# Loading keys and values through two DMA queues in a decode attention block

## The chip, the cores and the metric

The kernel runs on one core of a Trainium2 chip. The core has five engines that run side by side, each with its own stream of instructions: TensorE (PE, matrix products into PSUM), VectorE (DVE), ScalarE (ACT), GpSimd (POOL) and SyncE (SP, which here only issues transfers). Sixteen DMA engines move data between the chip's memory (HBM) and the core's on-chip memory (SBUF, 128 partitions). Instructions wait for each other through semaphores. A transfer raises its semaphore by 16 when it has landed. The metric is the device time of one execution in microseconds.

## The reference

A batch of four tokens goes through attention over cached keys and values and through a small mixer in parallel, and all is summed.

```python
xn = layernorm(x)                                   # x: (4, 1, 512)
q  = xn @ wq, cut into heads# (4, 32 heads, 1, 128)
scores = einsum("bhqd,bhkd->bhqk", q, k_cache) * 128 ** -0.5
o  = einsum("bhqk,bhkd->bhqd", softmax(scores), v_cache) -> (4, 1, 4096) @ wo
out = x + attention(xn) + mixer(xn)                 # mixer: xn + gelu(layernorm(xn) @ w3) @ w4
```

(Only one token stands in each sequence, so the mixer's shifts leave nothing of its first two matrices.) `k_cache` and `v_cache` have the shape (4, 32, 4096, 128) in float32: 268 MB each, read once. All other inputs together are about 24 MB. There is hardly any arithmetic for each byte.

## The kernel before

The 128 pairs of batch and head are worked in 32 **groups** of four heads (`NG = 32`, `HG = 4`). A group's keys are 8 MiB, laid out as 128 rows of 64 KiB, one row for each partition: partitions 0 to 31 hold the first head's keys, and so on. Its values have the same layout. SBUF holds three such slots: `KS[0]` and `KS[1]` take the keys of even and odd groups in turn, `S2` takes the values of every group. `S2` also holds, before the loop, the weights `wq`; `KS[1]` (`S0`) holds the layer norm's intermediates before that, so that its first keys wait for `d_T`, the signal that the queries `Q` are ready.

What each engine does for a group, in a loop of its own:

- **VectorE** spreads the group's queries over the partitions (L337, L340), waits for the keys (`s_k[n]`), multiplies them by the query in two halves (L343, L345), sums each product over the 128 elements (L347), then signals `k_free`, takes the maximum (L349 to L352) and signals `d_a`. For the first group the second half of the keys is a load of its own, and L345 waits for it (`s_h`, passed on by GpSimd).
- **ScalarE** waits for `d_a` and takes the exponentials, four instructions and their sums (`weights`, L245), which TensorE waits for (`a_p`). It then waits for TensorE's products and copies them out of PSUM (`values`, L233), waits for the sums and copies the group's result (`outputs`, L253). Its loop takes one group a turn; in the last turn it also has two instructions of the mixer (L261, L264).
- **TensorE** waits for the values (`s_v`) and the exponentials and makes 32 products with the values as moving operand, then signals `v_free` with the first product of the sums.
- **SyncE** issues every load but that of x (which ScalarE issues), in the order of its stream: `wq` in two pieces (L127, L128), the first group's keys in two halves (L130), then, after `d_T`, K1 (L119), V0 (L123), K2, V1, K3 and so on: each K load after `k_free`, each V load after `v_free`. At the end come `w3` (L146), `w4` (L148, L153), the last values in two pieces (L150, L152) and `wo` in six pieces (L157).

A transfer that is issued waits for nothing more; it stands in its queue behind those that the same engine issued earlier. The semaphores of the loads are taken back to zero by the one who waits (`take`), so each counts one load at a time. The names K*g* and V*g* below are the keys and values of group *g*.

Of the kernel before, what the change touches and what calls it, by code (L numbers as in the profile page):

```python
# [20 lines left out]
def decode_block(ctx: ExitStack, tc: tile.TileContext, x, k, v, wq, wo, w3, w4, out):  # L21
# [48 lines left out]
    def take(e, s, n=1):  # L70
        e.wait_ge(s, n).then_inc(s, -n)  # L71
# [26 lines left out]
    V = S2[:, :].rearrange("p (a j h d) -> p a h j d", a=C // 16, j=4, h=4)  # L98
    wo_sb = S0[:, :].rearrange("p (c n) -> p c n", c=WC)

    def part(t):
        return slice(t * P, (t + 1) * P)

# [7 lines left out]
    with tc.tile_critical(no_gpsimd_drain=True), nc.Block(no_gpsimd_drain=True) as block:  # L111

        @block.sync
        def _(e):
            def src(flat, g):
                return flat[g] if isinstance(g, int) else flat[bass.ds(g, 1)].rearrange("g p r -> (g p) r")

            def load_k(g, n):
                e.dma_start(KS[n][:, :], src(kf, g)).then_inc(s_k[n], 16)  # L119

            def load_v(g):
                take(e, v_free)
                e.dma_start(S2[:, :], src(vf, g)).then_inc(s_v, 16)  # L123

            FIRST, REST = slice(0, GF * 4 * DH), slice(GF * 4 * DH, ROW)
            wq_r = wq.rearrange("(p c) n -> p (c n)", p=P)
            e.dma_start(S2[:, FIRST], wq_r[:, FIRST]).then_inc(s_v, 16)  # L127
            e.dma_start(S2[:, REST], wq_r[:, REST]).then_inc(s_q, 16)  # L128
            for half, s in ((slice(0, ROW // 2), s_k[0]), (slice(ROW // 2, ROW), s_kh)):
                e.dma_start(S1[:, half], kf[0][:, half]).then_inc(s, 16)  # L130
            e.wait_ge(d_T, 1)
            load_k(1, 1)
            with nc.Fori(0, NG, 2, engines=[ET.SP]) as g:
                load_v(g)
                take(e, k_free)
                e.br_lt(g, NG - 2, on_true="sp_more", on_false="sp_next")
                with nc.body("sp_more", valid_engines=[ET.SP]):
                    after = nc.s_assert_within(g + 2, None, NG - 2,
                                               skip_runtime_bounds_check_because="the last turn skips this block")
                    load_k(after, 0)  # L140
                    load_v(after - 1)
                    take(e, k_free)
                    load_k(after + 1, 1)
                    nc.br("sp_next", engines=[ET.SP])
                nc.switch_bb("sp_next")
            e.dma_start(w3_sb, w3.rearrange("(p c) f -> p c f", p=P)).then_inc(s_w3, 16)  # L146
            w4_r = w4.rearrange("(p m) n -> p m n", p=P)
            e.dma_start(w4_sb[:, 0:4, :], w4_r[:, 0:4, :]).then_inc(s_w4, 16)  # L148
            e.wait_ge(v_half, NG)
            e.dma_start(S2[:, FIRST], vf[NG - 1][:, FIRST]).then_inc(s_v, 16)  # L150
            take(e, v_free)
            e.dma_start(S2[:, REST], vf[NG - 1][:, REST]).then_inc(s_q, 16)  # L152
            e.dma_start(w4_sb[:, 4:NF, :], w4_r[:, 4:NF, :]).then_inc(s_w4, 16)  # L153
            take(e, k_free)
            wo_r = wo.rearrange("(p c) n -> p c n", p=P)
            for n, (c0, c1) in enumerate(PIECES):
                e.dma_start(wo_sb[:, c0:c1, :], wo_r[:, c0:c1, :]).then_inc(s_wo[n], 16)  # L157
# [20 lines left out]
        @block.tensor  # L178
        def _(e):
            pe = [ET.PE]  # L180
            zero = e.zero_reg
            e.br_lt(zero, 0, on_true="pe_near", on_false="pe_far")
            with nc.body("pe_near", valid_engines=pe):
                with nc.Fori(0, NG + 1, 1, engines=pe) as g:
                    e.br_lt(g, NG, on_true="pe_turn", on_false="pe_mlp")
                    with nc.body("pe_mlp", valid_engines=pe):
                        e.wait_ge(s_w3, 16)
                        for c in range(NC):
                            for t in range(4):
                                i = mm(e, pb[32 * t:32 * t + 32, :FT], x1T[:, c, :], w3_sb[:, c, t * FT:(t + 1) * FT],  # L190
                                       c == 0, c == NC - 1)
                        i.then_inc(p_a, 1)
                        nc.br("pe_turn", engines=pe)
                    nc.switch_bb("pe_turn")
                    take(e, s_v, 16)
                    take(e, a_p)
                    for n in range(G4):
                        if n == GF:
                            take(e, v_rest)
                        t = n % 4  # L200
                        i = mm(e, pv[32 * t:32 * t + 32, :], pw[:, n, :], V[:, n // 4, t], n < 4, n >= G4 - 4)
                        if n == GF - 1:
                            i.then_inc(v_half, 1)
                    i.then_inc(p_a, 1)
                    mm(e, oz[:, HG:2 * HG], ones[:, :], rs[:, :], True, True).then_inc(v_free, 1)
                    take(e, a_p)
                    for m in range(4):
                        i = mm(e, oz[:, 0:HG], os[:, m, :], sel[:, HG * m:HG * m + HG], m == 0, m == 3)
                    i.then_inc(p_a, 1)
                e.br_lt(zero, 0, on_true="pe_far", on_false="pe_rest")  # L210
            with nc.body("pe_far", valid_engines=pe):
                e.br_lt(zero, 0, on_true="pe_rest", on_false="pe_near")
            nc.switch_bb("pe_rest")
            mm(e, total[:, 0:P], ident[:, :], base[:, :], True, False)
            e.wait_ge(s_w4, 32)
            take(e, d_p)
            for m in range(NF):
                t = m % 4
                mm(e, y[32 * t:32 * t + 32, :], gT[:, 32 * m:32 * m + 32], w4_sb[:, m, :], m < 4, False)
            take(e, d_p)  # L220
            mm(e, pb[:, 0:P], perm[:, :], Xt[:, :], True, True).then_inc(p_d, 1)

        @block.scalar
        def _(e):
            take(e, g_a)
            e.dma_start(xs[0:B, :], x.rearrange("b s d -> (b s) d")).then_inc(s_x, 16)
            for _ in range(2):
                take(e, d_a)
                e.activation(st[:, 2:3], st[:, 1:2], AF.Sqrt, bias=st[:, 3:4], scale=1.0 / D).then_inc(a_d, 1)

            def values():
                take(e, p_a)
                return e.copy(os[:, :, :], pv[:, :].rearrange("p (m d) -> p m d", m=4)).then_inc(a_p, 1)  # L233

            values()
            e.drain().then_inc(a_d, 1)
            take(e, p_a)
            e.activation(warm[:, :], st[:, 3:4], AF.Exp)

            def weights():  # L240
                take(e, d_a)
                for h in range(HG):
                    r = slice(32 * h, 32 * h + 32)
                    o = pw[r, :, 0:16].rearrange("p (a t) (w h) -> p a t w h", t=4, h=HG)[:, :, :, :, h]
                    i = e.activation(o, sc[r, :].rearrange("p (a w t) -> p a t w", w=4, t=4), AF.Exp, bias=st[r, 1:2], scale=1.0,  # L245
                                     accum_out=rs[r, h:h + 1])
                i.then_inc(a_p, 1)
                e.drain().then_inc(a_d, 1)

            def outputs(o):  # L250
                values()
                take(e, p_a)
                return e.copy(o, oz[:, 0:2 * HG].unsqueeze(1))  # L253

            act = [ET.Activation]
            with nc.Fori(0, NG, 1, engines=act) as g:
                weights()
                e.br_lt(g, NG - 1, on_true="act_values", on_false="act_mlp")
                with nc.body("act_mlp", valid_engines=act):
                    take(e, p_a)  # L260
                    e.copy(hs.rearrange("p (m i) -> p m i", i=32),  # L261
                           pb[:, :FT].rearrange("p (i m) -> p m i", i=32)).then_inc(a_d, 1)
                    take(e, d_a)
                    e.activation(gt, gu, AF.Tanh, scale=GELU_A).then_inc(a_d, 1)  # L264
                    nc.br("act_values", engines=act)
                nc.switch_bb("act_values")
                outputs(OS[:, bass.ds(g, 1), :])
            e.drain().then_inc(a_d, 1)

        @block.vector  # L270
        def _(e):
# [62 lines left out]
            with nc.Fori(0, NG, 2, engines=[ET.DVE]) as g:  # L334
                for n in range(2):
# [2 lines left out]
                                      Q[:, bass.ds(g + n, 1), :].rearrange("p o h -> p (o h)").unsqueeze(2)  # L338
                                      .to_broadcast([P, 4, 32])))
                    own(e.transpose(qb[:, :], qx[:, :]))  # L340
                    take(e, s_k[n], 16)
                    qw = qb[:, :].unsqueeze(1).to_broadcast([P, C // 2, DH])
                    mark(e.tensor_tensor(out=K[:, :C // 2, :], in0=K[:, :C // 2, :], in1=qw, op=ALU.mult))  # L343
                    take(e, s_h)
# [84 lines left out]
```

## Time and profile before

| what | value |
|---|---|
| time, median of 3 runs | 1305.1 us (1304.54 to 1305.36) |
| span of the profiled execution | 1302.8 us |
| the runs' median over that span | 2.3 us |
| DMA traffic | 561.05 MB, 431 GB/s over the span |
| busy: VectorE | 1167.5 us (90%) |
| busy: TensorE, matrix products | 371.5 us (29%) |
| busy: ScalarE | 107.5 us (8%) |

The profile is one execution recorded on the chip. The profiled execution's own time is given as its span, from the first to the last instruction; the times of the runs lie 2.3 us over it. Rows in order of time have the start in us, the duration in us, the engine, the line, the operation, what is written and read, and in brackets how long the engine had been idle and what ended that; SPq and ACTq are the queues of instructions of SyncE and ScalarE, in which a DMA row is the time of issuing and not that of moving the data. DMA queues are numbered: q1 holds what SyncE issues, q10 what ScalarE issues.

### The profile page before, as it was taken

How to read it: one execution, taken by the hardware profiler on the slowest of the kernel's cores; microseconds unless marked ns; L12 is line 12 of the kernel's file. 1: busy time of each engine (PE TensorE's matmuls, PEld its weight loads, DVE VectorE, ACT ScalarE, POOL GpSimd, SP SyncE). 2: the span in 40 equal slices, each digit the busy share in tenths (PEclk: the TensorE clock that was granted, in tenths of full speed). 3: DMA queues.
4: the chain of work that ended last, by engine and by line, in shares of the span. 5: the costliest groups of instructions: out<-in, count | busy, mean ns of one | idle time of the engine just before them, and what ended most of it. 6: DMA issues, size and time to landing. Idle time of an engine off the chain costs nothing. (4 is left out here: it accounts for less than half of the span.)

```text
span 1302.8 us, 7122 instructions
## 1 busy us (share of the span) xinstructions
PE 371.5 (29%) x2608; PEld 131.0 (10%) x2608; DVE 1167.5 (90%) x337; ACT 107.5 (8%) x330; POOL 2.5 (0%) x10
## 2 busy tenths in 40 slices
PE   3032123333113333212333212333311333321356
PEld 1010001111001111001111000111100111100112
DVE  4999999999999999999999999999999999999970
ACT  1000000000000000000000000000000000000010
POOL 0000000000000000000000000000000000000000
PEclk9565566666566666556666556666656666656678
DMA  9999999999999999999999999999999999999998
GB/s 402 436 449 421 449 421 449 421 439 429 425 445 421 449 421 449 421 449 421 449 421 445 425 437 431 425 445 421 449 421 449 421 449 421 447 423 445 425 430 344
DMA packets 11115, 561.05 MB, mean 431 GB/s; under 512 B 1244, under 2 KB 1252, under 8 KB 1640
## 3 DMA queue, kind: packets, MB, share of 16 engines
q1 hardware_dynamic: 11096, 561.00, 99.6%
q8 instruction: 2, 0.03, 0.0%
q14 instruction: 1, 0.01, 0.0%
q10 hardware_dynamic: 16, 0.01, 0.0%
HBM read 561.00 MB, written 0.01 MB: 431 GB/s over the span
## 5 line engine op out<-in xcount | busy, mean ns | idle before, releaser
L108 PE MATMUL ps<-slot,pw 128*32 128x512 f32 x2112 | 310.8, 753 | 905.5 <-PEq L71 905.5
L347 DVE TENSOR_REDUCE sc<-slot 128x128 f32<-128x16384 f32 x32 | 551.0, 17220 | 4.2
L343 DVE TENSOR_TENSOR slot<-slot,qb 128x8192 f32<-128x8192 f32 x32 | 278.1, 8692 | 60.8 <-DVEq L71 60.1
L345 DVE TENSOR_TENSOR slot<-slot,qb 128x8192 f32<-128x8192 f32 x32 | 277.9, 8684 | 1.1 <-DVEq L71 1.1
L108 PEld LDWEIGHTS ps<-slot,pw 128*32 128x32 f32 x2112 | 84.5, 134 | 1105.3 <-issue 1105.3
L233 ACT COPY os<-ps 128x512 f32<-128x512 f32 x33 | 19.3, 585 | 898.1 <-ACTq L71 898.1
L245 ACT ACTIVATE pw<-sc,st 32x128 f32<-32x128 f32 x128 | 67.4, 527 | 211.6 <-ACTq L71 210.4
L108 PE MATMUL ps<-sel,os 128*128 128x4 f32 x264 | 33.9, 252 | 18.6 <-PEq L71 18.6
L108 PEld LDWEIGHTS ps<-sel,os 128*128 128x128 f32 x264 | 31.9, 191 | 20.5 <-issue 20.5
L245 ACT ACTIVATION_READ_ACCUMULATOR pw<-sc,st 32x1 f32 x128 | 23.5, 184 | 0.0
L364 DVE RECIPROCAL rec<-OS 128x128 f32<-128x128 f32 x1 | 1.0, 952 | 15.5 <-DVEq L71 15.5
L349 DVE TENSOR_REDUCE st<-sc 128x1 f32<-128x128 f32 x32 | 9.2, 286 | 4.7
L108 PE MATMUL ps<-rs,ones 128*128 128x4 f32 x66 | 12.7, 263 | 0.0
L108 PEld LDWEIGHTS ps<-rs,ones 128*128 128x128 f32 x66 | 9.8, 188 | 27.7 <-issue 27.7
L337 DVE COPY qx<-Q 128x128 f32 x32 | 7.3, 227 | 5.0 <-issue 4.7
L391 DVE COPY res<-ps 64x128 f32<-64x128 f32 x1 | 0.3, 283 | 12.7 <-PE ps L108 12.7
L340 DVE STREAM_TRANSPOSE qb<-qx 128x128 f32<-128x128 f32 x32 | 10.0, 312 | 1.1
L108 PE MATMUL ps<-slot,X 128*4 128x512 f32 (+1 forms) x94 | 9.0, 457 | 3.9 <-DMA slot<-in_A_wo_dram 3.9
L253 ACT COPY OS<-ps 128x8 f32 x32 | 5.3, 165 | 43.8 <-ACTq L71 43.8
L351 DVE STREAM_TRANSPOSE mt<-mx 128x32 f32<-128x32 f32 x32 | 6.8, 211 | 1.1
L352 DVE TENSOR_REDUCE st<-mt 128x1 f32<-128x32 f32 x32 | 5.9, 186 | 1.1
L350 DVE COPY mx<-st 128x32 f32<-128x32 f32 x32 | 5.8, 181 | 1.1
(57 smaller groups left out, 39.3 us busy)
## 6 DMA issues: line engine op xcount, KB each, us to landing
slot<-in_A_k_cache_dram SPq DMA_DIRECT2D x2, 4096.0 KB, 36.0
slot<-in_A_wq_dram SPq DMA_DIRECT2D x1, 5120.0 KB, 22.4
slot<-in_A_v_cache_dram SPq DMA_DIRECT2D x1, 5120.0 KB, 20.5
slot<-in_B_w_dram SPq DMA_DIRECT2D x1, 3584.0 KB
slot<-in_A_wo_dram SPq DMA_DIRECT2D x1, 3584.0 KB, 29.4
slot<-in_A_wq_dram SPq DMA_DIRECT2D x1, 3072.0 KB, 10.7
slot<-in_A_v_cache_dram SPq DMA_DIRECT2D x1, 3072.0 KB, 13.1
slot<-in_B_w_dram SPq DMA_DIRECT2D x1, 2560.0 KB, 26.3
```

Source lines behind the costliest of these rows:

```text
L108: return e.matmul(o, l, r, start=start, stop=stop)
L233: return e.copy(os[:, :, :], pv[:, :].rearrange("p (m d) -> p m d", m=4)).then_inc(a_p, 1)
L245: i = e.activation(o, sc[r, :].rearrange("p (a w t) -> p a t w", w=4, t=4), AF.Exp, bias=st[r, 1:2], scale=1.0, accum_out=rs[r, h:h + 1])
L337: own(e.tensor_copy(qx[:, :].rearrange("p (h r) -> p h r", h=4), Q[:, bass.ds(g + n, 1), :].rearrange("p o h -> p (o h)").unsqueeze(2) .to ...
L340: own(e.transpose(qb[:, :], qx[:, :]))
L343: mark(e.tensor_tensor(out=K[:, :C // 2, :], in0=K[:, :C // 2, :], in1=qw, op=ALU.mult))
L345: own(e.tensor_tensor(out=K[:, C // 2:, :], in0=K[:, C // 2:, :], in1=qw, op=ALU.mult))
L347: mark(e.reduce_sum(sc[:, :], K, axis=AX.X))
L349: own(e.reduce_max(st[:, 0:1], sc[:, :], axis=AX.X))
L350: own(e.tensor_copy(mx[:, :], st[:, 0:1].to_broadcast([P, 32])))
L351: own(e.transpose(mt[:, :], mx[:, :]))
L352: e.tensor_reduce(st[:, 1:2], mt[:, :], axis=AX.X, op=ALU.max, negate=True).then_inc(d_a, 1)
```

## The change

Each load of a K or V slot becomes two transfers of 4 MiB: the even partitions, issued by SyncE at the place where the whole load stood, and the odd partitions, issued by ScalarE. Both raise the same semaphore, and the waits for it go from 16 to 32. ScalarE issues the odd half of K*g+2* in `weights` of group *g*, after `d_a` and ahead of the exponentials, and the odd half of V*g+1* in `outputs` of group *g*, after the copy of `values`. The odd halves of K1 and V0 come before its loop, after `d_T`. Its loop takes two groups a turn, since the K slot alternates; the last two groups, which have no loads to issue, are written out in a branch of their own with the mixer's two instructions.

Three other loads meet the same waits: the first pieces of `wq`, of K0 and of V31. SyncE issues each of them in two transfers, even and odd partitions, one after the other. The second pieces, and `w3`, `w4`, `wo`, stay whole.

```diff
--- before.py
+++ after.py
@@ -98,6 +98,15 @@
     V = S2[:, :].rearrange("p (a j h d) -> p a h j d", a=C // 16, j=4, h=4)
     wo_sb = S0[:, :].rearrange("p (c n) -> p c n", c=WC)
 
+    def parity(ap, n):
+        return ap.rearrange("(q two) r -> q two r", two=2)[:, n, :]
+
+    def source(flat, g):
+        return flat[g] if isinstance(g, int) else flat[bass.ds(g, 1)].rearrange("g p r -> (g p) r")
+
+    def load_half(e, slot, flat, g, n, s):
+        e.dma_start(slot[n::2, :], parity(source(flat, g), n)).then_inc(s, 16)
+
     def part(t):
         return slice(t * P, (t + 1) * P)
 
@@ -112,22 +121,21 @@
 
         @block.sync
         def _(e):
-            def src(flat, g):
-                return flat[g] if isinstance(g, int) else flat[bass.ds(g, 1)].rearrange("g p r -> (g p) r")
-
             def load_k(g, n):
-                e.dma_start(KS[n][:, :], src(kf, g)).then_inc(s_k[n], 16)
+                load_half(e, KS[n], kf, g, 0, s_k[n])
 
             def load_v(g):
                 take(e, v_free)
-                e.dma_start(S2[:, :], src(vf, g)).then_inc(s_v, 16)
+                load_half(e, S2, vf, g, 0, s_v)
 
             FIRST, REST = slice(0, GF * 4 * DH), slice(GF * 4 * DH, ROW)
             wq_r = wq.rearrange("(p c) n -> p (c n)", p=P)
-            e.dma_start(S2[:, FIRST], wq_r[:, FIRST]).then_inc(s_v, 16)
+            for n in range(2):
+                e.dma_start(S2[n::2, FIRST], parity(wq_r[:, FIRST], n)).then_inc(s_v, 16)
             e.dma_start(S2[:, REST], wq_r[:, REST]).then_inc(s_q, 16)
-            for half, s in ((slice(0, ROW // 2), s_k[0]), (slice(ROW // 2, ROW), s_kh)):
-                e.dma_start(S1[:, half], kf[0][:, half]).then_inc(s, 16)
+            for n in range(2):
+                e.dma_start(S1[n::2, :ROW // 2], parity(kf[0][:, :ROW // 2], n)).then_inc(s_k[0], 16)
+            e.dma_start(S1[:, ROW // 2:], kf[0][:, ROW // 2:]).then_inc(s_kh, 16)
             e.wait_ge(d_T, 1)
             load_k(1, 1)
             with nc.Fori(0, NG, 2, engines=[ET.SP]) as g:
@@ -147,7 +155,8 @@
             w4_r = w4.rearrange("(p m) n -> p m n", p=P)
             e.dma_start(w4_sb[:, 0:4, :], w4_r[:, 0:4, :]).then_inc(s_w4, 16)
             e.wait_ge(v_half, NG)
-            e.dma_start(S2[:, FIRST], vf[NG - 1][:, FIRST]).then_inc(s_v, 16)
+            for n in range(2):
+                e.dma_start(S2[n::2, FIRST], parity(vf[NG - 1][:, FIRST], n)).then_inc(s_v, 16)
             take(e, v_free)
             e.dma_start(S2[:, REST], vf[NG - 1][:, REST]).then_inc(s_q, 16)
             e.dma_start(w4_sb[:, 4:NF, :], w4_r[:, 4:NF, :]).then_inc(s_w4, 16)
@@ -192,7 +201,7 @@
                         i.then_inc(p_a, 1)
                         nc.br("pe_turn", engines=pe)
                     nc.switch_bb("pe_turn")
-                    take(e, s_v, 16)
+                    take(e, s_v, 32)
                     take(e, a_p)
                     for n in range(G4):
                         if n == GF:
@@ -235,10 +244,14 @@
             values()
             e.drain().then_inc(a_d, 1)
             take(e, p_a)
+            e.wait_ge(d_T, 1)
+            load_half(e, KS[1], kf, 1, 1, s_k[1])
+            load_half(e, S2, vf, 0, 1, s_v)
             e.activation(warm[:, :], st[:, 3:4], AF.Exp)
 
-            def weights():
+            def weights(load):
                 take(e, d_a)
+                load()
                 for h in range(HG):
                     r = slice(32 * h, 32 * h + 32)
                     o = pw[r, :, 0:16].rearrange("p (a t) (w h) -> p a t w h", t=4, h=HG)[:, :, :, :, h]
@@ -247,24 +260,34 @@
                 i.then_inc(a_p, 1)
                 e.drain().then_inc(a_d, 1)
 
-            def outputs(o):
+            def outputs(o, load):
                 values()
+                load()
                 take(e, p_a)
                 return e.copy(o, oz[:, 0:2 * HG].unsqueeze(1))
 
             act = [ET.Activation]
-            with nc.Fori(0, NG, 1, engines=act) as g:
-                weights()
-                e.br_lt(g, NG - 1, on_true="act_values", on_false="act_mlp")
-                with nc.body("act_mlp", valid_engines=act):
+            with nc.Fori(0, NG, 2, engines=act) as g:
+                e.br_lt(g, NG - 2, on_true="act_more", on_false="act_last")
+                with nc.body("act_more", valid_engines=act):
+                    on = nc.s_assert_within(g + 2, None, NG - 2,
+                                            skip_runtime_bounds_check_because="the last turn skips this block")
+                    for n in range(2):
+                        weights(lambda: load_half(e, KS[n], kf, on + n, 1, s_k[n]))
+                        outputs(OS[:, bass.ds(on - 2 + n, 1), :], lambda: load_half(e, S2, vf, on - 1 + n, 1, s_v))
+                    nc.br("act_turned", engines=act)
+                with nc.body("act_last", valid_engines=act):
+                    weights(lambda: None)
+                    outputs(OS[:, NG - 2:NG - 1, :], lambda: None)
+                    weights(lambda: None)
                     take(e, p_a)
                     e.copy(hs.rearrange("p (m i) -> p m i", i=32),
                            pb[:, :FT].rearrange("p (i m) -> p m i", i=32)).then_inc(a_d, 1)
                     take(e, d_a)
                     e.activation(gt, gu, AF.Tanh, scale=GELU_A).then_inc(a_d, 1)
-                    nc.br("act_values", engines=act)
-                nc.switch_bb("act_values")
-                outputs(OS[:, bass.ds(g, 1), :])
+                    outputs(OS[:, NG - 1:NG, :], lambda: None)
+                    nc.br("act_turned", engines=act)
+                nc.switch_bb("act_turned")
             e.drain().then_inc(a_d, 1)
 
         @block.vector
@@ -338,7 +361,7 @@
                                       Q[:, bass.ds(g + n, 1), :].rearrange("p o h -> p (o h)").unsqueeze(2)
                                       .to_broadcast([P, 4, 32])))
                     own(e.transpose(qb[:, :], qx[:, :]))
-                    take(e, s_k[n], 16)
+                    take(e, s_k[n], 32)
                     qw = qb[:, :].unsqueeze(1).to_broadcast([P, C // 2, DH])
                     mark(e.tensor_tensor(out=K[:, :C // 2, :], in0=K[:, :C // 2, :], in1=qw, op=ALU.mult))
                     take(e, s_h)
```

ScalarE's stream ahead of its loop, before and in the changed kernel (`ga`, `da`, `pa`, `dT` are the semaphores `g_a`, `d_a`, `p_a`, `d_T`; L108 of the changed kernel is `load_half`):

```order
L226 DMA slot<-in_A_x_dram 4x512 [waits ga]
L229 ACT_TABLE_LOAD [waits da]
L229 ACTIVATE st<-st 128x1
L229 ACTIVATE st<-st 128x1 [waits da]
L233 COPY os<-ps 128x512 [waits pa]
L238 ACT_TABLE_LOAD [waits pa]
L238 ACTIVATE warm<-st 128x1
L256 UNCONDITIONAL_BRANCH
```

```order
L235 DMA slot<-in_A_x_dram 4x512 [waits ga]
L238 ACT_TABLE_LOAD [waits da]
L238 ACTIVATE st<-st 128x1
L238 ACTIVATE st<-st 128x1 [waits da]
L242 COPY os<-ps 128x512 [waits pa]
L108 DMA slot<-in_A_k_cache_dram 64x16384 [waits pa,dT]
L108 DMA slot<-in_A_v_cache_dram 64x16384
L250 ACT_TABLE_LOAD
L250 ACTIVATE warm<-st 128x1
L270 UNCONDITIONAL_BRANCH
```

Two transfers of 64 rows, K1's and V0's odd halves, have come in after the first copy, with a wait for the queries (`dT`) at the first of them; the loading of the activation table stands behind them.

ScalarE's loop, before one group a turn, and in the changed kernel two (the rows of `act_more`, up to the branch at its end):

```order
L245 ACTIVATE pw,rs<-sc,st 32x32x4 [waits da]
L245 ACTIVATE pw,rs<-sc,st 32x32x4 x3
L258 COMPARE_AND_BRANCH
L261 COPY slot<-ps 128x448 [waits pa]
L264 ACTIVATE slot<-slot 128x448 [waits da]
L265 UNCONDITIONAL_BRANCH
L233 COPY os<-ps 128x512 [waits pa]
L253 ISA [waits pa]
L253 COPY OS<-ps 128x8
L256 REGISTER_ALU
L256 COMPARE_AND_BRANCH
```

```order
L108 ISA [waits da]
L108 DMA slot<-in_A_k_cache_dram 64x16384
L258 ACTIVATE pw,rs<-sc,st 32x32x4 x4
L242 COPY os<-ps 128x512 [waits pa]
L108 ISA
L108 DMA slot<-in_A_v_cache_dram 64x16384
L267 ISA [waits pa]
L267 COPY OS<-ps 128x8
L108 ISA [waits da]
L108 DMA slot<-in_A_k_cache_dram 64x16384
L258 ACTIVATE pw,rs<-sc,st 32x32x4 x4
L242 COPY os<-ps 128x512 [waits pa]
```

A K transfer stands at the head of each group's exponentials, behind the wait for `d_a`, and a V transfer between the copy of TensorE's products and the wait for the sums. The rows of the mixer have moved to the branch for the last turn.

SyncE's stream from its first load to the first loads of the loop (`vf` and `kf` are `v_free` and `k_free`):

```order
L127 DMA slot<-in_A_wq_dram 128x6144
L128 DMA slot<-in_A_wq_dram 128x10240
L130 DMA slot<-in_A_k_cache_dram 128x8192 x2
L119 DMA slot<-in_A_k_cache_dram 128x16384 [waits dT]
L133 UNCONDITIONAL_BRANCH
L123 ISA [waits vf]
L123 DMA slot<-in_A_v_cache_dram 128x16384
```

```order
L134 DMA slot<-in_A_wq_dram 64x6144 x2
L135 DMA slot<-in_A_wq_dram 128x10240
L137 DMA slot<-in_A_k_cache_dram 64x8192 x2
L138 DMA slot<-in_A_k_cache_dram 128x8192
L108 DMA slot<-in_A_k_cache_dram 64x16384 [waits dT]
L141 UNCONDITIONAL_BRANCH
L108 ISA [waits vf]
L108 DMA slot<-in_A_v_cache_dram 64x16384
```

The order of the loads is the same. What was one transfer of 128 rows is, for the first piece of `wq` and the first half of K0, two of 64 rows here; K1 and V0 have 64 rows here, and their other 64 stand in ScalarE's stream above. The second half of K0 keeps its 128 rows.

## The prediction

> **What bounds the kernel now.** I read the page first (the span in slices, the queues, the chain that ended last), then the windows of two middle groups, then the waits, and last the start and one group in order of time.
>
> ```profile
> span 1302.8 us, 7122 instructions
> DMA  9999999999999999999999999999999999999998
> DMA packets 11115, 561.05 MB, mean 431 GB/s; under 512 B 1244, under 2 KB 1252, under 8 KB 1640
> q1 hardware_dynamic: 11096, 561.00, 99.6%
> q10 hardware_dynamic: 16, 0.01, 0.0%
> DMA slot<-in_A_wo_dram 3%; PE ps L108 0%; SPq L157 0%; DVE res L391 0%
> ```
>
> The first queue, SyncE's, keeps the 16 DMA engines busy for 99.6% of the span, and the chain ends in a transfer. The other one is ScalarE's: 16 packets in all. Every K and V byte goes through SyncE's queue, and no slice of the span has a hole. The middle shows the same rate, group after group:
>
> ```profile
> 488.50:527.20 38.70, 11.26 (x74) 3.90 (x74) 35.85 (x10) 3.17 (x10) 0.00 (x0) 0.59 1.00 434
> 527.20:565.90 38.70, 10.69 (x74) 3.81 (x74) 35.91 (x10) 3.17 (x10) 0.00 (x0) 0.59 1.00 434
> DVE slot L343 <- DVEq L71: 60.1, 27, 2.4
> ACT os L233 <- ACTq L71: 898.1, 33, 29.9
> PE ps L108 <- PEq L71: 924.2, 68, 51.7
> ```
>
> In a window's row stand its length, the busy time of TensorE, its weight loads, VectorE, ScalarE and GpSimd, the granted clock, the DMA share and GB/s. A group is 38.70 us. Its 16.78 MB (two loads of 8 MiB, 128 rows of 64 KiB each) at 434 GB/s take 38.7 us: the period is the transfer time. The DMA share is 1.00. VectorE works 35.9 us of it and waits up to 2.4 us for the next K; TensorE and ScalarE wait most of the time. So only two things can move the time: the rate, and time in which the DMA engines have nothing queued. What is queued when can be read from one group:
>
> ```profile
> 518.00 0.58 ACT L233 COPY os<-ps 128x512 f32<-128x512 f32 x1 [29.89 <-ACTq L71]
> 518.41 0.33 SPq L123 DMA_DIRECT2D slot<-in_A_v_cache_dram  x1
> 523.50 0.33 SPq L119 DMA_DIRECT2D slot<-in_A_k_cache_dram  x1
> 524.35 0.53 ACT L245 ACTIVATE pw<-sc,st 32x128 f32<-32x128 f32 x1 [4.23 <-ACTq L71]
> 527.17 8.69 DVE L343 TENSOR_TENSOR slot<-slot,qb 128x8192 f32<-128x8192 f32 x1 [2.43 <-DVEq L71]
> 546.64 9.35 PE L108 MATMUL ps<-slot,pw 128*32 128x512 f32 x64 [26.88 <-PEq L71]
> ```
>
> K of the next group lands at 527.17 (VectorE starts). The V load issued at 518.41 runs behind it and lands at 546.64 (TensorE starts), then the K load of 523.50 runs. V is thus issued 8.8 us before the queue would run dry, and K 23.1 us before.
>
> **The change in the loop.** The bytes, the 64 KiB rows and the engines stay; the rows of a load come from two queues. ScalarE gets a K half and a V half in each group. Its K half is issued at the head of `weights`, ahead of the exponentials (524.35), about 0.9 us after SyncE's half (523.50); its V half after the copy of `values` (518.00 + 0.58 = 518.6), 0.2 us after SyncE's. Against the 23.1 and 8.8 us of backlog both are hidden. Behind the K issue on ScalarE stand the four exponentials, and TensorE waits for those; an issue of 0.56 us (ScalarE's load of x, below) makes them that much later. What hides it is V: TensorE starts only at 546.64, some 20 us after the exponentials. Without that cover it would be 31 × 0.56 = 17 us. The wait for 32 instead of 16 ends with the later half; both run at the same time over the same engines, so it ends when the whole load did. VectorE's 2.4 us a group is spare. The loop body of two groups saves a branch or so on an engine that waits: nothing.
>
> The 65 added transfers (62 loads and three first halves that SyncE issues in two pieces) add 65 × 16 = 1040 completion writes, if each transfer still runs on 16 engines. The price of one has no row. Bounds: 561.05 MB at the windows' 434 GB/s are 1292.7 us, while the engines were busy 99.6% of 1302.8 = 1297.6 us; those 4.9 us cover the slow first packets, all short rows and today's 1244 packets under 512 B. So 1040 more cost at most 4.9 × 1040 / 1244 = 4.1 us, at least nothing. I take **0.5 us**, near the lower end, since the start and the short rows have their part of the 4.9.
>
> **The change at the start.** This is where I expect time to go.
>
> ```profile
> 0.97 0.41 SPq L127 DMA_DIRECT2D slot<-in_A_wq_dram  x1
> 1.60 0.56 ACTq L226 DMA_DIRECT2D slot<-in_A_x_dram  x1
> 7.92 1.28 DVE L295 COPY slot<-slot 4x512 f32<-4x512 f32 x3 [4.65 <-DVEq L71]
> 30.79 0.33 SPq L119 DMA_DIRECT2D slot<-in_A_k_cache_dram  x1
> 31.54 0.35 SPq L123 DMA_DIRECT2D slot<-in_A_v_cache_dram  x1
> 33.69 8.69 DVE L343 TENSOR_TENSOR slot<-slot,qb 128x8192 f32<-128x8192 f32 x1 [2.03 <-DVEq L71]
> 43.51 8.69 DVE L345 TENSOR_TENSOR slot<-slot,qb 128x8192 f32<-128x8192 f32 x1 [1.13 <-DVEq L71]
> 52.34 17.22 DVE L347 TENSOR_REDUCE sc<-slot 128x128 f32<-128x16384 f32 x1
> 69.96 0.34 SPq L119 DMA_DIRECT2D slot<-in_A_k_cache_dram  x1
> 82.24 9.44 PE L108 MATMUL ps<-slot,pw 128*32 128x512 f32 x64 [51.74 <-PEq L71]
> 92.23 0.33 SPq L123 DMA_DIRECT2D slot<-in_A_v_cache_dram  x1
> 106.26 0.33 SPq L119 DMA_DIRECT2D slot<-in_A_k_cache_dram  x1
> slot<-in_A_wq_dram SPq DMA_DIRECT2D x1, 3072.0 KB, 10.7
> ```
>
> Now one queue holds wq, K0 in two halves (33.69 and 43.51 are their landings), and from 31 us on K1 and V0 behind them. VectorE multiplies a K0 half as it lands, reduces, and frees the slot at 69.96, when K2 is issued. V0 lands at 82.24. K2 is issued 12.3 us before everything else has landed; that is the only cover the start has.
>
> In the changed kernel the odd halves of K1 and V0 (8 MiB) stand on ScalarE's queue at 31 us, while SyncE's queue still holds the second half of K0. They don't wait behind it: x, on ScalarE's queue, was issued after wq's 3 MiB and had landed by 7.92, and that part of wq landed only at 0.97 + 10.7 = 11.7. So the queues interleave, and K0's second half has to share.
>
> How late does it get? A row of that half is 32 KiB, a row of ScalarE's loads 64 KiB. *Upper end:* row for row, each of its 128 rows has a row of ScalarE's 8 MiB with it. Then 12.58 MB instead of 4.19 MB go after 33.69: 29.0 instead of 9.7 us, 19.3 us later. *Lower end among shares:* byte for byte, 4.19 MB more, 9.7 us later. Rows of SyncE's that are already under way when ScalarE's arrive go first; each round of 16 of them takes 16 rows of 64 KiB off the delay, 1.05 MB or 2.4 us. x gives a size: from the end of its issue (2.16) to 7.92 it took 5.8 us. Starting and landing cost at most 3.4 us (wq's 10.7 less 3.15 MB at 434 GB/s, 7.3), so some 2.4 us went behind wq's rows of 24 KiB, at 16 × 24 KiB in 0.9 us between two and three rounds, one of which may have been its completion's. I take row for row with two rounds ahead: 19.3 − 4.8 = 14.5 us.
>
> What is late next: the second product (43.51 to 58.0), the reduction, the slot, and SyncE's K2, 69.96 to 84.5. The engines meanwhile get the same total, so everything queued still lands at 82.2. Of the 12.3 us of cover I take off the 3.4 us of starting and landing: 8.9 us are left. The DMA engines then stand empty for 14.5 − 8.9 = **5.6 us**, once. Ends: 19.3 − 8.9 = 10.4 us, and 9.7 − 8.9 = 0.8 us. Is it paid again? V1 is issued 10 us after TensorE starts (82.24 to 92.23), inside K2's 19.4 us. K1's work takes 36.3 us (69.96 to 106.26), so K3 is issued at 84.5 + 36.3 = 120.8, and V1 lands at 82.2 + 5.6 + 38.7 = 126.5, later by more than the 3.4 of starting; each further group gains the 2.4 us of VectorE's slack. So no second hole; but the transfers bound the rest, so nothing gives the first one back.
>
> [...]
>
> At the end nothing changes its cover: ScalarE's last half is V30's, and w3 and w4 follow on SyncE's queue.
>
> ```profile
> 1243.26 9.20 PE L108 MATMUL ps<-slot,pw 128*32 128x512 f32 x64 [27.02 <-PEq L71]
> 1248.22 0.33 SPq L150 DMA_DIRECT2D slot<-in_A_v_cache_dram  x1
> ```
>
> V30 lands at 1243.26; the next two loads on SyncE's queue (w3's 3584 KB and 1024 KB of w4) hold the engines 10.9 us more at 434 GB/s, to 1254, and the next load is issued at 1248.22. Some 5 us are left if the two halves end a row (2.4 us) apart.
>
> **Sum.** Span 1302.8 + 5.6 + 0.5 = 1308.9. The runs' median, 1305.1, lies 2.3 us over the span, so **1311.2 us**, 0.5% slower. A measurement of this kernel tells about 0.2% (2.6 us) from no change.
>
> **Rivals.**
>
> *The start loses nothing.* If the share is byte for byte, or four and more rounds of K0 are ahead, K2 comes in time: 0 to 0.8 us of hole and 0.5 of completions, 1305.6 to 1306.4. For it: two to three rounds of x's wait, which may be more for longer rows. Against it: VectorE needs the last row of the slowest engine. [...]
>
> *Faster.* Two queues close gaps between rows that the windows don't resolve. The price at most is the idle 0.4% of the span, 5.2 us, which would come near to cancelling the hole (1306.0); only with no hole at the start is it 1300.4. Against it: a DMA share of 1.00 at 434 GB/s leaves no gap to close.
>
> [...]
>
> **Chances and range.** A hole at the start, as forecast: 0.58 (1307.5 to 1316). No hole: 0.22. Gaps closed: 0.08, of which 0.06 end faster. Crowded paths: 0.12, all slower. Faster 0.06, same 0.24 (the second case and what is left of the third), slower 0.70. The range is 1304.5 to 1316: it takes in the no-hole case, and above it the 10.4 us end with the 0.5; it leaves out the crowded case, a part of the faster one and the end where completions cost 4.1 us. The forecast's own range is 1307.5 to 1316.
>
> **What would show it.** In the changed profile the second K0 product should start near 58 us (52 to 63), K2 near 84.5, and one slice of the DMA row near 85 us should be below the rest; queue 10 should carry 260 MB. The middle groups should still take 38.7 us and 434 GB/s. If the second product starts at 53 us or before and K2 before 79, there is no hole and the time is unchanged. If a group takes other than 38.7 us, the rate moved, and the sum is wrong whatever the start does.

## The result, and the profile after

The changed kernel took 1307.63 us (median of 8 runs, 1305.99 to 1310.38), the kernel before in the same sets of runs 1304.63 us: 1.0024 times as long, with a 95% interval of 1.0016 to 1.0033. That is 3.0 us slower. The forecast had the side right and the size about twice too large (6.1 us).

The page of the changed kernel, the lines that answer to those shown of before:

```profile
span 1305.9 us, 7243 instructions
DMA packets 12156, 561.06 MB, mean 430 GB/s; under 512 B 2284, under 2 KB 2292, under 8 KB 2680
q1 hardware_dynamic: 7176, 300.95, 53.5%
q10 hardware_dynamic: 4976, 260.06, 46.0%
```

Queue 10 now carries 260 MB, and there are 1040 more packets under 512 B, as counted. Two groups in the middle, in the view by windows (length, busy times, granted clock, DMA share, GB/s):

```profile
493.90:532.60 38.70, 10.47 (x74) 3.73 (x74) 35.86 (x9) 3.18 (x11) 0.00 (x0) 0.63 1.00 434
532.60:571.30 38.70, 9.90 (x74) 3.63 (x74) 35.92 (x9) 3.17 (x11) 0.00 (x0) 0.63 1.00 434
```

A group takes 38.70 us at 434 GB/s as before. The rate did not move, and a load of 64 rows, every second partition, runs as fast as one of 128. What changed stands at the start, in order of time:

```profile
16.51 4.11 PE L117 MATMUL ps<-slot,pw 128*32 128x512 f32 x24 [16.51 <-PEq L71]
...
24.05 7.17 PE L117 MATMUL ps<-slot,pw 128*32 128x512 f32 x40 [3.43 <-PEq L71]
...
33.42 0.47 SPq L108 DMA_DIRECT2D slot<-in_A_k_cache_dram  x1
33.42 0.53 ACTq L108 DMA_DIRECT2D slot<-in_A_k_cache_dram  x1
33.98 0.82 ACTq L108 DMA_DIRECT2D slot<-in_A_v_cache_dram  x1
...
34.43 8.69 DVE L366 TENSOR_TENSOR slot<-slot,qb 128x8192 f32<-128x8192 f32 x1
...
53.16 8.69 DVE L368 TENSOR_TENSOR slot<-slot,qb 128x8192 f32<-128x8192 f32 x1 [10.03 <-DVEq L71]
...
79.61 0.47 SPq L108 DMA_DIRECT2D slot<-in_A_k_cache_dram  x1
...
80.58 0.51 ACTq L108 DMA_DIRECT2D slot<-in_A_k_cache_dram  x1
...
83.75 8.92 PE L117 MATMUL ps<-slot,pw 128*32 128x512 f32 x64 [50.62 <-PEq L71]
```

VectorE waits 10.03 us for K0's second half, which lands at 53.16 instead of 43.51. K2 is issued at 79.61 instead of 69.96, at about the time when everything queued has been moved. And one thing is new that the forecast did not have: K1 is issued at 33.42 instead of 30.79, because TensorE's second batch of query products takes 7.17 us. The kernel before, its timeline:

```profile
16.70 5.35 PE L108 MATMUL ps<-slot,pw 128*32 128x512 f32 x24 [16.70 <-PEq L71]
...
24.09 4.50 PE L108 MATMUL ps<-slot,pw 128*32 128x512 f32 x40 [2.04 <-PEq L71]
```

The clock that TensorE was granted stands in the view by windows, here before:

```profile
24.00:28.00 4.00, 3.91 (x40) 1.44 (x40) 0.00 (x0) 0.00 (x0) 0.00 (x0) 1.00 0.91 393
```

and in the changed kernel:

```profile
24.00:28.00 4.00, 3.95 (x20) 1.13 (x24) 0.00 (x0) 0.00 (x0) 0.00 (x0) 0.50 0.93 401
```

40 matmuls in four microseconds at 1.00, 20 at 0.50: over these four microseconds the second batch ran at half the clock.

The trace also records single DMA packets; here one packet is one row of a load (7936 packets of 64 KiB in both kernels, for 62 × 128 rows), or one completion write (16 more for each of the 65 added transfers). It doesn't name the engine, but linked into chains (a packet that begins as another ends) the packets give what one DMA engine moved. Over some 100 us the chains stay apart; over the whole kernel they don't, since engines often end a packet at the same moment. One engine of the changed kernel; each entry is the start in us, S or A for the queue of SyncE or ScalarE, and the size in KiB, c for a completion:

```
31.1 S32 | 32.3 S c | 32.3 S32 | 33.5 S32 | 34.7 S32 | 35.9 S32 | 37.1 S32 | 38.3 A64 | 40.7 S32 |
42.0 A64 | 44.4 S32 | 45.6 A64 | 48.0 S32 | 49.2 A64 | 51.6 S c | 51.6 A c | 51.6 S64 | 54.0 A64 |
56.5 S64 | 58.9 A64 | 61.3 S64 | 63.7 A64 | 66.1 S64 | 68.5 A64 | 71.0 ... | 80.6 S c | 81.0 S64
```

From the first A on the queues take turns, one packet each, 32 KiB (1.21 us) against 64 KiB (2.42 us). Eight S32 from 32.3 on are this engine's share of K0's second half; four A64 went between them, the last one ahead of the completion alone. 4 × 2.42 us = 9.7 us, which is the lateness of 53.16. Ahead of ScalarE's first row (38.3), which was issued at 33.42, five rows of that half went, the first of them already under way then. By the same packets fifteen of the engines stood empty near 80.5 us for 0 to 0.9 us, and one, the last to end, for 2.1 us (81.44 to 83.52); the mean of the 16 is 0.4 us. The first row of K2 that each engine then moved took 3.1 to 3.5 us instead of 2.42, which is 0.9 us more on average.

### The profile page after: what moved, and what is told of

It is laid out like the page before. It is cut to its first block, busy times and chain, and to the rows that moved or that the text cites. A ratio compares the mean times of both kernels' runs of the same rounds, so it can differ in the third digit from the quotient of the medians.

```text
span 1305.9 us, 7243 instructions
## 1 busy us (share of the span) xinstructions
PE 366.4 (28%) x2608; PEld 130.1 (10%) x2608; DVE 1167.6 (89%) x337; ACT 107.5 (8%) x330; POOL 2.5 (0%) x10
## 5 line engine op out<-in xcount | busy, mean ns | idle before, releaser
L117 PE MATMUL ps<-slot,pw 128*32 128x512 f32 x2112 | 305.7, 743 | 914.1 <-PEq L71 914.1
L366 DVE TENSOR_TENSOR slot<-slot,qb 128x8192 f32<-128x8192 f32 x32 | 278.2, 8692 | 54.7 <-DVEq L71 53.6
L267 ACT COPY OS<-ps 128x8 f32 (+1 forms) x32 | 5.3, 165 | 45.5 <-ACTq L71 45.5
```

Source lines behind the costliest of these rows:

```text
L117: return e.matmul(o, l, r, start=start, stop=stop)
```

## Experiments

Theory A is the forecast's: the hole near 80 us is what the change costs. Theory B says that it is the 65 added transfers, theory C that it is the use of two queues in every group. The kernel before ran beside each kernel below, with a median of 1304.75 to 1304.83 us.

### The changed kernel again

No edit. Eleven runs.

> The changed kernel once more, to see how far its start moves. Theory A (the hole at the start): the second product of K0 starts between 53 us (queries ready at 33.4 us, as in the changed kernel's profile) and 58 us (queries at 30.8 us), and the DMA engines stand empty for 0.5 to 5 us near 80 us; the time follows the hole, 1306 to 1310 us. Theory B (the added transfers) and theory C (two queues in every group) expect 1307.6 us whatever the start does.

Median 1307.69 us, 1.0021 [1.0012, 1.0030]. Three rows in order of time:

```profile
32.33 0.53 ACTq L108 DMA_DIRECT2D slot<-in_A_k_cache_dram  x1
...
55.46 8.69 DVE L368 TENSOR_TENSOR slot<-slot,qb 128x8192 f32<-128x8192 f32 x1 [13.23 <-DVEq L71]
...
81.91 0.47 SPq L108 DMA_DIRECT2D slot<-in_A_k_cache_dram  x1
```

Two windows of the same profile. A packet counts whole in the window in which it begins, so the DMA share can pass 1, and 0.00 means that none began:

```profile
80.00:82.00 2.00, 0.00 (x0) 0.00 (x0) 1.82 (x3) 0.00 (x0) 0.00 (x0) 0.50 0.00 0
82.00:84.00 2.00, 0.00 (x0) 0.00 (x0) 1.76 (x6) 0.57 (x2) 0.00 (x0) 0.50 1.45 492
```

With queries 1.1 us earlier, K0's second half is 2.3 us later, and between 80 and 82 us no packet begins. Fifteen engines moved four rows of ScalarE's between those of K0's second half, as above; one moved five and ended 2.8 us after the last of them (54.7 against 51.9), and VectorE waits for all. By the chains all engines were empty, for 1.9 to 3.9 us (2.8 us on average). The profiled run took 1307.76 us, as long as the one above (1307.67) though most of its engines were empty for longer. Probably the one engine with 2.1 us set the end there, and all of them here; the chains can't be followed to the end of the kernel to show it. The eleven times lie in three heaps, 1305.7 to 1305.9, 1307.5 to 1308.2 and 1310.0 to 1310.2 us. The median of 1307.69 us fits theories B and C as well; what they don't have is the hole.

### The first odd halves from SyncE

```diff
             load_k(1, 1)
+            load_half(e, KS[1], kf, 1, 1, s_k[1])
+            load_half(e, S2, vf, 0, 1, s_v)
...
-            load_half(e, KS[1], kf, 1, 1, s_k[1])
-            load_half(e, S2, vf, 0, 1, s_v)
```

> SyncE issues the odd halves of K1 and V0 too; all later ones stay with ScalarE. Theory A: K0's second half lands at 43.5 us again, K2 is issued near 70 us, no hole; 1305.5 to 1306.5 us, 1 to 2 us under the changed kernel. Theories B and C: as the changed kernel, 1307.6 us, since the loop is the same.

1306.02 us, 1.0009 [1.0000, 1.0018]: 1.6 us of the 3.0 are gone, 1.2 us are left. Its rows in order of time:

```profile
43.53 8.69 DVE L368 TENSOR_TENSOR slot<-slot,qb 128x8192 f32<-128x8192 f32 x1 [1.14 <-DVEq L71]
...
70.96 0.55 ACTq L108 DMA_DIRECT2D slot<-in_A_k_cache_dram  x1
...
89.50 9.06 PE L117 MATMUL ps<-slot,pw 128*32 128x512 f32 x64 [57.31 <-PEq L71]
...
99.11 0.47 SPq L108 DMA_DIRECT2D slot<-in_A_v_cache_dram  x1
```

One of its windows:

```profile
98.00:100.00 2.00, 1.44 (x16) 0.89 (x8) 2.00 (x1) 0.58 (x1) 0.00 (x0) 1.00 0.08 33
```

K0 is in time and the hole at 80 us is gone. But K2's odd half (70.96) has an empty queue and now overtakes V0, all of which stands on SyncE's: V0 lands at 89.50 instead of 82.24, V1 is issued at 99.11 instead of 92.23, and the engines run dry near 99 us (0.08), for 0.4 us on average by the packets. The first rows after that took 0.7 us more than 2.42 us on average; together this is 1.1 us, and the span grew by 1.0 (1303.8 against 1302.8). So what is left may be the same mechanism at another load, or theory C. The next two runs tell.

### All halves from SyncE

Each `load_half` of SyncE stands in a loop over both halves; ScalarE issues none.

```diff
-                load_half(e, KS[n], kf, g, 0, s_k[n])
+                for m in range(2):
+                    load_half(e, KS[n], kf, g, m, s_k[n])
...
-                        weights(lambda: load_half(e, KS[n], kf, on + n, 1, s_k[n]))
+                        weights(lambda: None)
```

> All halves are issued by SyncE, one after the other; ScalarE issues none. The added transfers and completions stay, the second queue is gone. Theory B: 1307 to 1307.6 us, as the changed kernel. Theory A: no hole, 1305.1 to 1306.5 us. Theory C: near the kernel before, 1304.6 to 1305.3 us, with the last rows of the slowest engine 1 us nearer to the others' than in the changed kernel.

1304.72 us, 1.0000 [0.9991, 1.0009]. The added transfers and completions cost nothing that can be measured: theory B is out. The time lies in theory C's band and a little under theory A's, so this run alone doesn't part those two.

### ScalarE's first halves after K0 has landed

```diff
             e.wait_ge(d_T, 1)
+            e.wait_ge(s_h, 1)
             load_half(e, KS[1], kf, 1, 1, s_k[1])
```

> ScalarE issues the odd halves of K1 and V0 only after K0's second half has landed; all else as in the changed kernel. If the hole near 80 us is what the change costs, K0's second product starts at 43.5 us, K2 is issued near 70 us, V0 lands near 82 us (not near 89 us as where SyncE issued the first odd halves), no engine is empty before the end, and the time is 1304.7 to 1305.3 us. If two queues in every group cost something of their own, it stays near 1306 us, as with the first odd halves on SyncE's queue.

1304.93 us, 1.0000 [0.9991, 1.0009]: one wait makes the two queues cost nothing. Its rows in order of time:

```profile
43.59 0.53 ACTq L108 DMA_DIRECT2D slot<-in_A_k_cache_dram  x1
...
43.64 8.69 DVE L369 TENSOR_TENSOR slot<-slot,qb 128x8192 f32<-128x8192 f32 x1 [1.14 <-DVEq L71]
...
70.09 0.47 SPq L108 DMA_DIRECT2D slot<-in_A_k_cache_dram  x1
...
86.42 8.94 PE L117 MATMUL ps<-slot,pw 128*32 128x512 f32 x64 [54.12 <-PEq L71]
```

The window in which the changed kernel's engines ran dry:

```profile
80.00:82.00 2.00, 0.00 (x0) 0.00 (x0) 2.00 (x2) 0.00 (x0) 0.00 (x0) 0.50 1.22 524
```

K2 is issued at 70.09, packets begin in 80 to 82 us, and no chain has a gap before the last loads. V0 lands 4 us late (86.42, expected near 82), for which the cover suffices. Every group still has two queues, so theory C is out as well, and with it the second reading of the 1.2 us above.

### Twice the rows in K0's second half

```diff
-            e.dma_start(S1[:, ROW // 2:], kf[0][:, ROW // 2:]).then_inc(s_kh, 16)
+            for n in (2, 3):
+                q = slice(n * ROW // 4, (n + 1) * ROW // 4)
+                e.dma_start(S1[:, q], kf[0][:, q]).then_inc(s_kh, 16)
...
-            take(e, s_kh, 16)
+            take(e, s_kh, 32)
```

> The second half of K0 comes in two transfers with rows of 16 KiB instead of one with rows of 32 KiB: the same bytes, twice the rows. If the queues share row for row, more of ScalarE's 64 KiB rows come between them: K0's second product starts at 58 to 63 us instead of 53, the hole grows by 5 to 10 us, 1312 to 1318 us. If they share byte for byte, nothing changes: 53 us and 1307.6 us.

1315.10 us (4 runs), 1.0075 [1.0059, 1.0090]: the same bytes in rows half as long, and 7.5 us more than the changed kernel. Two rows in order of time:

```profile
63.05 8.69 DVE L370 TENSOR_TENSOR slot<-slot,qb 128x8192 f32<-128x8192 f32 x1 [20.57 <-DVEq L71]
...
89.50 0.47 SPq L108 DMA_DIRECT2D slot<-in_A_k_cache_dram  x1
```

Two of its windows:

```profile
82.00:84.00 2.00, 0.00 (x0) 0.00 (x0) 2.00 (x1) 0.00 (x0) 0.00 (x0) 0.50 0.00 0
...
88.00:90.00 2.00, 0.00 (x0) 0.00 (x0) 1.77 (x4) 0.00 (x0) 0.00 (x0) 0.50 0.00 0
```

All eight of ScalarE's rows for each engine now fit between those of K0: 8 × 2.42 = 19.4 us, and 63.05 is 19.5 us over 43.51. The engines stand empty from 80.5 to over 90 us, 9.1 to 11.1 us by the chains, 10.2 us on average. That settles the unit of the share. It also gives the cover: 19.5 us late, 10.2 us empty, so 9.3 us.

### Why are the queries late?

The changed kernel's queries came 1.4 to 2.6 us later than before's. Two more profiles, of the kernel before and of the changed one, and two edits on that: the changed kernel with `wq`'s first piece in one transfer; and the kernel before with only that piece in two (GpSimd passes the landing on in the last two).

> The kernel before once more, for the time at which its queries are ready. If that moves with the granted clock from run to run, SyncE's K1 is issued somewhere from 30.8 to 33.5 us; K2 is issued at 70 us all the same, and the time stays 1304.5 to 1305.4 us. If the later queries of the changed kernel came from the change, K1 is issued at 30.8 us again.

> The changed kernel a third time. K0's second product should lie on a ladder with steps of 2.4 us (one 64 KiB row of ScalarE's for each engine): 53.2 us with queries at 33.4 us, 55.5 us at 32.3 us, 57.9 us at 31 us; and K2's issue 26.45 us after it.

```diff
-            for n in range(2):
-                e.dma_start(S2[n::2, FIRST], parity(wq_r[:, FIRST], n)).then_inc(s_v, 16)
+            e.dma_start(S2[:, FIRST], wq_r[:, FIRST]).then_inc(s_first, 16)
```

> The changed kernel with the first piece of wq in one transfer again (GpSimd passes its landing on to TensorE, as it does for the other pieces). In all kernels that split this piece x landed 0.2 to 0.7 us earlier, TensorE's first products started earlier, the gap to its second batch was over 2.4 us, the granted clock fell within that batch, and the queries were ready at 32.2 to 33.4 us; in the two looks at the kernel before they were ready at 30.8. If the split does that, queries come at 30.8 us here, more of K0's rows then lie behind ScalarE's: K0's second product at 55.5 to 58 us, a hole of 3 to 5.5 us, 1308 to 1311 us, slower than the changed kernel. If the clock only happens to fall so, queries stay at 32 to 33.5 us and the time at 1307.6 us.

```diff
-            e.dma_start(S2[:, FIRST], wq_r[:, FIRST]).then_inc(s_v, 16)
+            for n in range(2):
+                half = wq_r[:, FIRST].rearrange("(q two) r -> q two r", two=2)[:, n, :]
+                e.dma_start(S2[n::2, FIRST], half).then_inc(s_first, 16)
```

> The kernel before with only the first piece of wq in two transfers of even and odd partitions. If that is what makes the queries late, x lands before 7.8 us, SyncE's K1 is issued at 32.2 to 33.4 us instead of 30.8, and nothing follows: K2 at 70 us, 1304.5 to 1305.4 us, because one queue has no hole to lose. If not, K1 is issued at 30.8 us.

The kernel before, profiled again (1304.88 us), its timeline:

```profile
24.20 4.50 PE L108 MATMUL ps<-slot,pw 128*32 128x512 f32 x40 [2.14 <-PEq L71]
...
30.90 0.33 SPq L119 DMA_DIRECT2D slot<-in_A_k_cache_dram  x1
```

The kernel before with `wq`'s first piece split (1304.49 us; x landed at 6.68 us instead of 7.92), its timeline:

```profile
23.92 5.82 PE L109 MATMUL ps<-slot,pw 128*32 128x512 f32 x40 [3.54 <-PEq L71]
...
31.95 0.33 SPq L120 DMA_DIRECT2D slot<-in_A_k_cache_dram  x1
```

The changed kernel with that piece whole (1307.96 us, 1.0022 [1.0013, 1.0031]; x landed at 7.80 us), its timeline:

```profile
24.29 6.20 PE L118 MATMUL ps<-slot,pw 128*32 128x512 f32 x40 [2.42 <-PEq L71]
...
32.67 0.47 SPq L109 DMA_DIRECT2D slot<-in_A_k_cache_dram  x1
...
53.58 8.69 DVE L370 TENSOR_TENSOR slot<-slot,qb 128x8192 f32<-128x8192 f32 x1 [11.00 <-DVEq L71]
```

So in the kernel before the queries came 1.1 us late with the split (31.95, a little under the 32.2 expected; one profile, and GpSimd's passing on of the landing came in with the split), and in the changed kernel they are late without the split as well. For the whole piece the first branch of the expectation, that the split does it, failed in each of its numbers; queries and time came out as in the second. The other profile of the changed kernel (1306.50 us) had queries at 32.22, and K0's second half at 53.18, a step of the ladder, but not the one that I had put to such queries (55.5): here no engine moved a fifth row of ScalarE's. What goes with the lateness in all these rows is the idle time in brackets: TensorE's gap between its first batch and its second, which waits for `wq`'s rest near 24 us. With 2.04 and 2.14 us the second batch took 4.50 us, with 2.42 us and more 5.8 to 7.2. Two things make the gap. x lands 0.1 to 1.2 us earlier in these kernels, so TensorE's first batch begins earlier; and that batch itself is often shorter. In the changed kernel's own profile the second is the larger part: the batch began 0.19 us earlier (16.51 against 16.70) and took 1.24 us less (4.11 against 5.35), though the granted clock reads 1.00 from 16 to 22 us in both; why, stays open. The next run makes the gap smaller by letting x land later.

### x later

```diff
+            e.wait_ge(c_done, 2)
             e.dma_start(xs[0:B, :], x.rearrange("b s d -> (b s) d")).then_inc(s_x, 16)
```

> The changed kernel with ScalarE's load of x issued after GpSimd's second signal, 1.3 us later. So far the queries came at 30.8 us where TensorE's gap ahead of its second batch was 2.04 and 2.14 us, and at 32.0 to 33.4 us where it was 2.42 us or more, with the clock granted at half in that batch. If the gap does it, x lands near 9 us, the gap is under 2 us, the second batch takes 4.5 us and the queries are ready near 30.8 us, as the prediction had assumed. Then K0's second product starts at 55.5 to 58 us, the engines stand empty for 3 to 5.5 us, and the time is 1308.5 to 1311 us, over the changed kernel's 1307.6. If the gap does nothing, queries stay at 32 to 33.5 us and the time at 1307.6 us.

Median 1309.08 us (6 runs, 1307.38 to 1309.96), 1.0030 [1.0017, 1.0042]; the profiled run took 1309.95 us. Its rows in order of time:

```profile
24.23 4.50 PE L117 MATMUL ps<-slot,pw 128*32 128x512 f32 x40 [1.45 <-PEq L71]
...
30.92 0.53 ACTq L108 DMA_DIRECT2D slot<-in_A_k_cache_dram  x1
...
57.39 8.69 DVE L369 TENSOR_TENSOR slot<-slot,qb 128x8192 f32<-128x8192 f32 x1 [14.86 <-DVEq L71]
...
83.83 0.47 SPq L108 DMA_DIRECT2D slot<-in_A_k_cache_dram  x1
```

The clock over the second batch, and the window before K2's issue:

```profile
24.00:28.00 4.00, 3.77 (x36) 1.44 (x40) 0.45 (x2) 0.00 (x0) 0.00 (x0) 1.00 0.97 418
...
82.00:84.00 2.00, 0.00 (x0) 0.00 (x0) 1.82 (x3) 0.00 (x0) 0.00 (x0) 0.50 0.00 0
```

With the gap at 1.45 us the clock stays at 1.00, the queries are ready at 30.9 us, as the forecast had assumed, and its steps are then nearly met: K0's second product at 57.4 (58.0 in the forecast), K2 at 83.8 (84.5), the engines empty for 3.5 to 5.4 us, 4.6 us on average (5.6). The earlier signal to ScalarE (30.9 us against 32.3 and 33.4) came with a longer hole (4.6 us against 2.8 and 0.4). That it makes the kernel slower is likely but not beyond noise: the interval, 1.0017 to 1.0042, overlaps the changed kernel's, 1.0016 to 1.0033.

## Why the prediction was right and wrong

**The bound, and the loop at no cost: right.** Groups take 38.70 us at 434 GB/s in both kernels; ScalarE's issues are hidden. The kernel in which only the start differs from the changed one is as fast as before (1.0000).

**The added completions, 0.5 us: somewhat high.** With all halves on one queue no difference could be measured (1304.72 against 1304.83 us), and the bounds of 0 to 4.1 us held.

**The hole at the start: right in kind.** K0's second half shares, VectorE is late, K2 is late, the engines run dry once near 80 us, and nothing gives it back (the span is 3.1 us longer); take the sharing away and the cost is gone (1.0000 with ScalarE's first halves after K0).

**Row for row: right.** No row of before showed the unit of the share; row for row was the author's choice between two values, and the runs showed it. Byte for byte would have left the kernel with the short rows unchanged; it lost 7.5 us more. The chains show the turns, one packet each, with packets of 64 KiB against 32 KiB in the changed kernel and against 16 KiB with the short rows, and show that a completion waits its turn too: in the chain above the half's last row ends at 49.2, ScalarE's row goes next, and the completion comes at 51.6.

**The cover of 8.9 us: right.** It is the lateness less the mean empty time: 9.3 us in the kernel with short rows (19.5 − 10.2) and with x later (13.9 − 4.6), 9.1 in the changed kernel's second profile (11.95 − 2.84).

**The lateness of 14.5 us: this is the step that failed.** It was 9.7 us in the changed kernel's profile, 12.0 and 9.7 in its two other profiles. The forecast took the queries' time from the trace of before, 30.8 us, as though the change could not move it. It moved to 32.2 to 33.4, by when more of K0's rows were through, and fewer of ScalarE's could come between. With the queries put back to 30.9 us the lateness was 13.9 us. The forecast's "two rounds ahead" hung on the same time: in the changed kernel five rows of the half went first, four in its two other profiles (three on the engine of the second that landed last). With queries at 30.9 us it was three on fifteen engines and two on the one that landed last, on which six of ScalarE's rows came between, as the forecast had counted.

**The sum.** 5.6 us of hole were expected. The engine that was empty for longest was so for 2.1 us in the changed kernel's profile; when it was profiled again all were, for 2.8 us on average, and for 4.6 us with early queries. The span grew by 3.1 us in each of the first two (1305.9 against 1302.8) and by 5.4 in the last (1308.2). The empty time is not all of that. In every profile with a hole the engines' first rows after it took 0.6 to 0.9 us more than 2.42 us on average, while in the two profiles of the kernel before no row of 64 KiB took over 2.6 us. The forecast had put this restart at nothing. With it the holes nearly account for the spans: 4.6 + 0.7 against 5.4 with early queries, 10.2 + 0.7 against 10.9 with short rows, 2.8 + 0.7 against 3.1 in the second profile; for the one late engine of the first, 2.1 + 1.1 against 3.1. So it is in part luck that the forecast's 6.1 us come near the 5.4 of early queries: the restart, which it lacked, stands where its 0.5 us of completions and a little too much hole had stood.

**The rivals.** No hole: every profile in which ScalarE issues its first odd halves as soon as the queries are ready has one near 80 us. Closed gaps: no, the rate stayed at 434 GB/s. Crowded paths, by which the forecast meant a lower rate of loads of 64 rows: no, a group of such loads took 38.70 us at 434 GB/s, as before.

**Left open.** Why one engine began K2 2.3 us after the fifteen others in the changed kernel's profile, and two began it 1.0 to 1.3 us after the others in its third; why the first rows after a hole are slow; and what exactly in the changed start makes x land earlier and the first batch of products shorter, since the queries are late with `wq`'s first piece whole as well.

## What to carry to other kernels

Here, with the DMA engines busy for 99.6% of the span in the kernel before, a second queue brought no bandwidth (434 GB/s either way); it only changed who goes first. A load on the empty queue overtook what stood on the other one, row for row, twice (K0's second half, which landed at 53.16 us instead of 43.51, and V0 where SyncE issued the first odd halves, at 89.50 instead of 82.24). So look for a load that is needed next and has another queue's long rows beside it; a wait of one instruction was enough here. And before a delay is sized from the old trace, ask whether the change moves the event from which it is counted.

## What had not been expected

- TensorE's second batch of query products took 4.50 us after idle gaps of 1.45, 2.04 and 2.14 us, and 5.8 to 7.2 us after 2.42 us and more. The clock stood at 1.00 over it in the first three, at 0.50 in the first four of the changed kernel's 7.17 us. With x 0.1 to 1.2 us earlier the queries were 1.1 to 2.6 us later.
- The queues' turns go by packets even where one has 64 KiB (2.42 us) and the other 16 KiB (0.6 us): ScalarE's queue then moved four times the bytes of SyncE's.
- The times of the changed kernel (19 timed runs) fall mostly into three heaps, near 1305.9, 1307.7 and 1310.2 us. That these are the steps of one 64 KiB row (2.42 us) is not shown: two profiles with K0's second half one step apart took 1307.67 and 1307.76 us.
